# A second order list for attention and feed-forward products: 384 and 512 tokens instead of 448 and 448

## The chip, the cores and the metric

The kernel runs on one core of a Trainium2 chip. The time is device time in microseconds (us) of one execution, from the start of the program to its end; of several executions the median is given. TensorE is called PE here, VectorE DVE, ScalarE ACT, GpSimd POOL and SyncE SP, as the profile calls them.

## The reference

Three layers follow one another, all in float32, for 2 batches of 448 tokens.

```python
# causal attention: 12 heads, 448 tokens, 64 dims
scores = matmul(q, k.T) / sqrt(64);  scores[upper triangle] = -1e9
attn = exp(scores - max);  attn = attn / (sum(attn) + 1e-9);  a = attn @ v
x = a.transpose(0, 2, 1, 3).reshape(2, 448, 768)
# feed-forward with token mixing
xk = mu_k * x + (1 - mu_k) * x_prev        # x_prev: x one token earlier
xr = mu_r * x + (1 - mu_r) * x_prev
x = sigmoid(xr @ w_r) * (maximum(xk @ w_k, 0) ** 2 @ w_v)   # 768 -> 1024 -> 768
# convolution feed-forward
h = maximum(x @ w_in, 0)                   # 768 -> 1024
out = (h * sigmoid(conv3(h, conv_w))) @ w_out               # 1024 -> 768
```

## The kernel before

The attention is cut into 12 jobs of two heads each (a head pair): jobs 0 to 5 are batch 0, jobs 6 to 11 batch 1. For a job, q and k are loaded (`Lk`, lines 281 to 286), transposed on PE (`kqT`, L300) and copied out of PSUM (`kC`, L307). The scores come in two parts (`sc`, L321), over row tiles of 64 queries, tile i against (i + 1) * 64 keys. For each of the 7 row tiles, DVE adds the mask and takes the maximum in one custom instruction (`red`, L334), ACT takes the exponential and sums it (`exp`, L343), and after the reciprocal (`rec`, L350 and L351) each tile is scaled (`norm`, on POOL, DVE or ACT). PE transposes p back in two groups a and b (`T`, L363), four copies of 512 columns bring that into SBUF (`C`, L372, on ACT or DVE), and PE multiplies with v (`V`, L391) into a bank called `po`. From `po` the token mixing follows: `mP` scales it by one factor (kind 0 into `mixed`, kind 1 into `m`), `mD` adds the shifted part (DVE), and `mH` and `mL` split the mixed tokens into a high and a low part, `xr`.

Every feed-forward product is three matmuls in a split float32 format, high by high, high by low, low by high (`mm3`, L64). A slice of 128 columns of a weight is loaded as 64-bit numbers (`w1:L`, L159), narrowed to float32 in steps a to e (a on ACT, b on POOL or DVE, the others on DVE), and split into high (`h`, ACT) and low (`l`). `w0` to `w5` are the six slices of w_r and `w6` to `w8` the first three of w_k. `pr e.b.c` is the product of w_r's slice e with the b-th part of the tokens and the c-th 128 rows (L563 to L569); six of them, c = 0 to 5, fill one PSUM bank, which `sr` copies out. `k x:H` and `k x:L` split `mixed` into the parts of `xk`, x = 6 * batch + c. `E0` to `E3` are the products of w_k's first two slices, each with 6 values of c: slice 0 with both parts of the tokens, then slice 1 (L599 to L603).

What sets the order is a list of such tokens, `ORDER` (from L500). It is issued token by token and PE, ACT, DVE and POOL run their instructions in just that order (L625); SP takes its DMAs in it too. A letter behind a slash is the engine: a is ACT, v is DVE, p is POOL. `W0` and `W*n` are matmuls on a constant early on. After the list the rest of the kernel follows (remaining w_k slices, w_v, w_in, convolution, w_out), ordered by the scheduler; its stages already use 512 and 384 columns. Below, the "tail" is the stretch in which only products are left on PE, between the last job's `V` and the end of the list.

Of the kernel before, what the change touches and what calls it, by code (L numbers as in the profile page):

```python
# [19 lines left out]
def kernel(  # L20
# [457 lines left out]
    class Slice:  # L478
# [27 lines left out]
        3:kC.k/a 2:sc.1 0:norm.5/p 0:C.bX/v 0:T.a 1:rec 2:red.6 1:norm.6/p 2:exp.3 3:sc.1 0:C.aX/a 2:exp.2 2:exp.5
        2:red.1 1:norm.0/p 3:sc.2 0:C.aY/v 4:kqT 1:norm.2/p 3:red.6 1:norm.5/p 2:exp.0 2:red.4 1:norm.4/p 2:exp.1
        1:norm.1/p 1:T.a 3:red.5 Wend 4:kC.k/v 3:red.0 w1:L 1:C.aY/v 2:exp.4 1:Lv 2:exp.6 1:norm.3/p 2:rec 3:exp.0
        0:V.b 1:T.b 4:kC.q/a 3:exp.6 2:norm.5/p 2:norm.1/p 4:sc.1 3:red.1 2:norm.3/p 3:exp.5 0:V.a 3:red.3 1:C.bY/v
        2:norm.6/p w1:a 2:norm.0/p 2:norm.2/p w1:b/p 3:red.2 3:red.4 1:C.bX/v 1:C.aX/v 4:red.4 3:exp.3 2:norm.4/p  # L510
        0:mP.1/a 5:Lk 3:exp.4 4:red.1 2:T.a 3:exp.2 4:sc.2 2:T.b 3:exp.1 0:mP.0/v 2:C.aX/a 4:red.6 2:C.aY/a 3:rec
        w1:c 3:norm.3/p 3:norm.0/p 5:kqT 4:exp.1 4:red.3 4:red.0 2:C.bX/v 4:exp.4 5:kC.k/v 0:mD.1 3:norm.5/p
        3:norm.1/p 4:red.2 1:V.a 5:kC.q/a 4:exp.0 1:V.b 5:sc.2 4:exp.3 4:red.5 4:exp.6 3:norm.2/p 3:norm.6/p 6:Lk
        0:mD.0 3:norm.4/p 5:red.0 0:mH/p 2:Lv 0:mL/p 6:kqT 5:red.2 2:C.bY/a 5:red.3 4:exp.5 5:red.5 7:Lk 3:Lv
        6:kC.q/a 3:T.a 4:exp.2 3:T.b 5:sc.1 3:C.aY/v w1:d 4:rec 6:kC.k/a 3:C.aX/a 3:C.bY/a 1:mP.1/a 4:norm.4/p
# [5 lines left out]
        3:mP.0/v w1:l/p 7:sc.2 9:Lk 7:sc.1 5:T.a 7:red.0 5:C.aY/a 6:exp.2 7:red.6 3:mD.1 7:red.5 6:exp.4 4:V.b
        5:norm.1/p 4:V.a 8:kqT 6:exp.0 7:exp.6 7:red.1 pr1.0.0 w2:L 3:mD.0 3:mH/p 6:rec pr1.0.1 7:red.4 2:mH/p
        6:norm.4/p 5:T.b 8:kC.q/a 7:red.2 7:exp.0 6:norm.5/p 5:C.aX/a 8:kC.k/a 7:red.3 4:mP.1/v 6:norm.6/p 9:kqT
        5:C.bY/v 7:exp.1 6:norm.0/p 9:kC.q/a 4:mP.0/a 5:C.bX/v 7:exp.5 7:exp.3 9:kC.k/v 8:sc.1 7:exp.2 8:red.6
        2:mL/p 8:sc.2 6:norm.1/p 6:T.a 8:red.3 5:V.a 8:red.4 3:mL/p 8:red.2 5:V.b w2:a 6:C.aY/v 6:norm.2/p 7:exp.4
        6:C.aX/a 6:norm.3/p 8:exp.6 4:mD.1 6:T.b 8:red.1 10:Lk 8:exp.2 4:mD.0 7:rec 8:exp.1 w2:b/p 7:norm.6/p w2:c
        10:kqT 8:red.5 pr1.0.2 10:kC.q/a 6:C.bX/a 8:red.0 w2:d 8:exp.0 7:norm.0/v pr1.0.3 4:mH/a 6:C.bY/a 7:norm.5/a
        9:sc.1 w2:e 6:Lv w2:h 10:kC.k/v 11:Lk 9:sc.2 9:red.5 9:red.6 5:mP.1/v 4:mL/p w2:l/p w3:L 8:exp.4 6:V.b 6:V.a
        8:exp.5 7:T.a 8:exp.3 9:red.3 9:red.2 9:red.1 7:norm.2/p 7:norm.1/p w0:L 5:mP.0/a 8:rec 7:C.aY/a pr1.0.4
        9:exp.5 9:exp.6 7:norm.4/v 5:mD.1 6:mP.1/a w3:a 5:mH/p pr2.0.0 5:mL/p 7:norm.3/v 8:norm.4/v pr2.0.1 9:red.0  # L530
# [533 lines left out]
```

## Time and profile before

| | us |
|---|---|
| median of three runs (354.3, 354.36, 353.45) | 354.3 |
| the profiled execution, its span | 351.6 |
| PE busy in it | 345.2 |
| DVE busy | 306.9 |
| ACT busy | 235.1 |
| POOL busy | 90.3 |

The profile is of one execution; its span is the time from its first to its last instruction, and all times in the rows are counted from its start. An engine is busy when an instruction of it runs; time in which it waits is idle time. Matmuls overlap in PE's pipeline, so its busy time counts overlapping ones once. Two rows that follow one another on an engine overlap a little too, so the price of an instruction in a full engine is the distance from its start to the next start.

### The profile page before, as it was taken

What the parts mean: (1) busy time and instruction counts of PE and PEld (TensorE: products, weight loads), DVE (VectorE), ACT (ScalarE), POOL (GpSimd) and SP (SyncE); (2) the same over time, 40 slices, a digit from 0 to 9 for tenths busy, and PEclk for the clock granted to TensorE, in tenths of its full rate; (3) what the DMA queues carried; (4) which work ended last, traced back from release to release, by engine and by line L of the source; (5) the groups of instructions that cost most, each with busy time, mean ns of one, the idle gap of its engine ahead of it and who ended that gap; (6) DMA issues with size and microseconds to landing.
All of it is one profiled execution on the core that took longest, in us unless ns stands there. A gap on an engine that the chain in (4) does not pass through costs nothing.

```text
span 351.6 us, 7196 instructions
## 1 busy us (share of the span) xinstructions
PE 345.2 (98%) x2682; PEld 309.2 (88%) x2682; DVE 306.9 (87%) x629; ACT 235.1 (67%) x515; POOL 90.3 (26%) x149
## 2 busy tenths in 40 slices
...
GB/s 132 146 222 144 127 222 213 90 116 93 7 95 106 66 180 181 121 148 240 142 187 171 156 101 173 179 143 128 89 103 79 89 2 0 67 134 202 138 91 135
DMA packets 63228, 45.33 MB, mean 129 GB/s; under 512 B 34752, under 2 KB 62156, under 8 KB 63192
## 3 DMA queue, kind: packets, MB, share of 16 engines
...
q10 hardware_dynamic: 928, 0.23, 0.3%
...
## 4 chain that ended last, share of the span: by engine, by line
PE 95%; DVE 1%; DMA 1%; POOL 1%; SPq 1%; issue 1%; ACT 0%; POOLq 0%
PE pk L66 17%; PE pv L66 17%; PE pr L66 13%; PE A L66 7%; PE po L391 6%; PE s L321 4%; PE B L66 4%; PE c L66 2%; PE Yb L363 2%; PE D L66 2%; PE Xa L363 2%; PE W L561 1%; PE q L300 1%; PE ph5l L66 1%; PE ph6l L66 1%; PE ph4l L66 1%
## 5 line engine op out<-in xcount | busy, mean ns | idle before, releaser
L887 POOL DMA_DIRECT2D s<-g x12 | 12.7, 1177 | 194.9 <-ACT st L87 188.6
L343 ACT ACTIVATE p<-e,st 128x448 f32<-128x448 f32 (+6 forms) x84 | 42.1, 507 | 1.7 <-DVE st L334 1.5
L72 POOL TENSOR_SCALAR p<-p,st 128x64 f32<-128x64 f32 (+6 forms) x70 | 34.6, 512 | 20.7 <-DVE st L334 11.4
L334 DVE CUSTOM_DVE_ANT_0 e<-s,mask 128x192 f32<-128x192 f32 (+6 forms) x84 | 31.6, 415 | 0.4 <-ACT p L343 0.2
L391 PE MATMUL po<-pt,v 128*64 128x128 f32 (+4 forms) x384 | 24.0, 277 | 0.0
L807 DVE SCALAR_TENSOR_TENSOR cv<-hT,cw,cv 128x448 f32<-128x448 f32 x32 | 21.5, 681 | 2.7 <-ACT cv L804 2.6
L391 PEld LDWEIGHTS po<-pt,v 128*64 128x64 f32 x384 | 20.0, 137 | 3.3 <-issue 0.3
L321 PE MATMUL s<-kT,qT 64*64 64x384 f32 (+6 forms) x336 | 22.1, 386 | 0.5 <-DVE kT L79 0.2
L321 PEld LDWEIGHTS s<-kT,qT 64*64 64x64 f32 x336 | 14.9, 132 | 6.6 <-ACT qT L79 0.7
L343 ACT ACTIVATION_READ_ACCUMULATOR p<-e,st 128x1 f32 x84 | 16.3, 194 | 0.0
L91 POOL TENSOR_TENSOR xr<-m,xr 128x448 fp32r<-128x448 f32 x10 | 12.0, 1198 | 2.1 <-ACT xr L87 1.7
L87 ACT ACTIVATE x<-xv 128x512 fp32r<-128x512 f32 (+1 forms) x12 | 6.8, 573 | 8.1 <-DVE xv L706 8.0
L811 ACT ACTIVATE cv<-cv 128x448 f32<-128x448 f32 x16 | 9.1, 571 | 3.2 <-DVE cv L807 3.2
L999 ACT ACTIVATE o<-A 128x384 f32<-128x384 f32 x3 | 1.5, 491 | 14.7 <-PE A L66 14.6
L804 ACT ACTIVATE cv<-hT,cw 128x448 f32<-128x448 f32 x16 | 10.7, 668 | 0.5 <-DVE g L91 0.3
L813 DVE TENSOR_TENSOR cv<-cv,hT 128x448 f32<-128x448 f32 x16 | 9.9, 621 | 1.2 <-ACT cv L811 1.2
L91 DVE TENSOR_TENSOR k<-a,k 128x512 fp32r<-128x512 f32 (+2 forms) x16 | 9.9, 619 | 0.0
L66 PE MATMUL pv<-k,wv0hl 128*128 128x512 f32 (+1 forms) x48 | 9.9, 364 | 0.0
L66 PE MATMUL pv<-k,wv4hl 128*128 128x512 f32 (+1 forms) x48 | 9.8, 363 | 0.0
L66 PE MATMUL pv<-k,wv2hl 128*128 128x512 f32 (+1 forms) x48 | 9.8, 363 | 0.0
L66 PE MATMUL pv<-k,wv3hl 128*128 128x512 f32 (+1 forms) x48 | 9.8, 363 | 0.0
L66 PE MATMUL pv<-k,wv5hl 128*128 128x512 f32 (+1 forms) x48 | 9.8, 363 | 0.0
...
## 6 DMA issues: line engine op xcount, KB each, us to landing
rqk<-in_q_dram SPq DMA_DIRECT2D x24, 112.0 KB, 2.8
rqk<-in_k_dram SPq DMA_DIRECT2D x22, 112.0 KB, 3.0
...
```

The lines of the kernel that those rows point to most:

```text
L66: nc.tensor.matmul(ps_out, x, y, start=first and i == 0, stop=last and i == 2, skip_group_check=more,)
L72: nc.gpsimd.tensor_scalar(out_, in_, s, 1.0, ALU.mult, ALU.mult)
L91: e.tensor_tensor(out_, x, f32(h), ALU.subtract)
L321: nc.tensor.matmul(held[self.name(f"s{f}")][1][h, o:z], qT[r, i * LO:(i + 1) * LO], kT[r, :(i + 1) * LO], start=True, stop=True,)
L334: nc.vector.tensor_tensor_reduce(t[:, :w], used(self.name(f"s{f}"))[:, o:z], mask[:, S - w:], -SCALE, 3e38, ALU.add, ALU.min, self.st[:, 0 ...
L343: nc.scalar.activation(p[:, :w], self.s[i][:, :w], AF.Exp, bias=self.st[:, 0, i:i + 1], scale=-1.0, accum_out=self.st[:, 1, i:i + 1],)
L363: nc.tensor.transpose(o[:, u * LO:(u + 1) * LO], self.p[i][r, k0:k0 + P], ident[r, r])
L391: nc.tensor.matmul(self.T["po"][j * D:(j + 1) * D, 1 + i * LO - z:1 + (i + n) * LO], self.v[:, kc, j], self.T["pt"][:, a - z:a + n * LO], ...
L804: nc.scalar.activation(a, x[:, 0:S], AF.Copy, scale=cw[:, f:f + 1])
L807: nc.vector.scalar_tensor_tensor(a, x[:, j:S + j], cw[:, j * NF + f:j * NF + f + 1], a, ALU.mult, ALU.add)
L813: (nc.gpsimd if eng == "p" else nc.vector).tensor_tensor(a, a, hc, ALU.mult)
L887: nc.gpsimd.dma_start(out=dst, in_=f32(x), accum_op=ALU.add)
```

## The change

The order list is replaced by another of the same 712 pieces of work: the same loads, scores, exponentials, products. What differs is their order and, for copies, scalings, mixing and splitting steps, the engine that does them. Job 9 now comes ahead of jobs 7 and 8. Each product of w_r and the two slices of w_k now takes tokens 0 to 383 (part 0) and 384 to 895 (part 1) instead of 448 and 448, and so do the copies `sr` and the first two w_k slices' squares. The E products run as E2, E0, E3, E1 instead of E0, E1, E2, E3. The first weight load, `w1:L`, stands behind job 5's `Lk` instead of in front of it.

```diff
     TOK = [slice(b * S, (b + 1) * S) for b in range(B)]
+    PART = [slice(0, 3 * P), slice(3 * P, NT)]
+
+    def width(t):
+        return t.stop - t.start
...
     ORDER = """
...
-        11:norm.6/p 11:norm.1/v 11:norm.5/a 10:C.aY/a 9:V.a 9:V.b 11:norm.4/p 11:norm.0/a 7:mH/p 10:C.bX/v 11:T.b
...
+        11:norm.2/p 11:norm.1/p 11:T.b 11:C.bY/a 11:C.bX/a 10:V.a w5:d w5:e w7:L 10:V.b 10:mP.1/a 10:mD.1 11:V.a
...
     def xr_products(e, b, c):
         if c == 0:
             bank(f"pr{e}_{b}", 1)
-        products(held[f"pr{e}_{b}"][1][:, :S], [slices[e].t], xr, TOK[b], NC, c)
+        t = PART[b]
+        products(held[f"pr{e}_{b}"][1][:, :width(t)], [slices[e].t], xr, t, NC, c)
...
-        copy(eng, sr[e][:, TOK[b]], used(f"pr{e}_{b}")[:, :S])
+        t = PART[b]
+        copy(eng, sr[e][:, t], used(f"pr{e}_{b}")[:, :width(t)])
...
             f, b = divmod(int(what[1:]), B)
-            pk_banks[f, b] = bank(f"pk{f}_{b}", 1)[:, :S]
+            t = PART[b]
+            pk_banks[f, b] = bank(f"pk{f}_{b}", 1)[:, :width(t)]
             for c in range(NC):
-                products(pk_banks[f, b], [slices[NE + f].t], [xk[i] for i in range(NC)], TOK[b], NC, c)
+                products(pk_banks[f, b], [slices[NE + f].t], [xk[i] for i in range(NC)], t, NC, c)
...
-        pks = [(TOK[b], pk_banks[f, b]) for b in range(B)] if f < 2 else token_mm(f"pk{f}", w, xk, False)
+        pks = [(PART[b], pk_banks[f, b]) for b in range(B)] if f < 2 else token_mm(f"pk{f}", w, xk, False)
```

Three places show how the instructions stand. The first is ACT at the end of the attention, in the kernel before; `p5_1` is a tile of probabilities that is scaled, `pt` the transposed p, `Xa_11` the PSUM bank of job 11's group a, `wr5c` a weight slice in step a, `m` and `mixed` the mixed tokens, `xr2` a high part.

```order
L76 ACTIVATE p5_1_137<-p5_1_137,st_144 128x384
L79 COPY pt_0_140<-Ya_10_1817 128x512
L76 ACTIVATE p0_1_121<-p0_1_121,st_144 128x64
L137 ACTIVATE wr5c_1900<-wr5raw_1735 128x768
L87 ACTIVATE xr2_108<-m_8_1730 128x448
L76 ACTIVATE m_9_1922<-po_9_1860,mu_98 128x448
L137 ACTIVATE wr4c_1926<-wr4raw_1750 128x768
L76 ACTIVATE mixed3_103<-po_9_1860,mu_98 128x448
L79 COPY pt_1_141<-Xa_11_1904 128x512
L76 ACTIVATE m_11_1976<-po_11_1950,mu_98 128x448
```

The same place on ACT after the change:

```order
L76 ACTIVATE p0_1_121<-p0_1_121,st_144 128x64
L76 ACTIVATE p6_1_139<-p6_1_139,st_144 128x448
L79 COPY pt_1_141<-Ya_10_1837 128x512
L79 COPY pt_1_141<-Xa_10_1836 128x512
L79 COPY pt_1_141<-Xb_10_1858 128x512
L79 COPY pt_1_141<-Yb_10_1859 128x512
L137 ACTIVATE wr5c_1887<-wr5raw_1735 128x768
L79 COPY pt_0_140<-Ya_11_1895 128x512
L79 COPY pt_0_140<-Xa_11_1894 128x512
L79 COPY pt_0_140<-Yb_11_1917 128x512
L79 COPY pt_0_140<-Xb_11_1916 128x512
L76 ACTIVATE m_10_1957<-po_10_1936,mu_98 128x448
```

All eight copies of the last two jobs are ACT's now, where five of them were DVE's, and the mixing steps and a weight step stand elsewhere.

The second place is SP's queue in the kernel before, around the first weight load; `rqk_4` are job 4's q and k, `v_1` is one of the buffers of v.

```order
L286 DMA rqk_4_393<-in_q_dram 64x7x64 x2
L286 DMA rqk_4_393<-in_k_dram 64x7x64 x2
L159 DMA wr1raw_517<-in_moe_w_r_dram 128x6x128
L292 DMA v_1_113<-in_v_dram 128x3x64 x2
L293 DMA v_1_113<-in_v_dram 64x2x64
L286 DMA rqk_5_602<-in_q_dram 64x7x64 x2
L286 DMA rqk_5_602<-in_k_dram 64x7x64 x2
```

The same place on SP after the change:

```order
L290 DMA rqk_4_450<-in_q_dram 64x7x64 x2
L290 DMA rqk_4_450<-in_k_dram 64x7x64 x2
L290 DMA rqk_5_461<-in_q_dram 64x7x64 x2
L290 DMA rqk_5_461<-in_k_dram 64x7x64 x2
L159 DMA wr1raw_639<-in_moe_w_r_dram 128x6x128
L296 DMA v_1_113<-in_v_dram 128x3x64 x2
L297 DMA v_1_113<-in_v_dram 64x2x64
```

Job 5's four issues for q and k went ahead of the weight load and of v's three.

The third place is PE at the first products, in the kernel before; `q_8` and `k_8` are job 8's transposes, `Yb_5` and `Xb_5` job 5's of p, `pr1_0` the bank of w_r's slice 1 and the first part of the tokens.

```order
L300 MATMUL q_8_1093<-ident_85,rqk_8_945 128x64
L300 MATMUL k_8_1094<-ident_85,rqk_8_945 128x64
L66 MATMUL pr1_0_1113<-xr0_106,wr1hl_971 128x448 x3
L66 MATMUL pr1_0_1113<-xr1_107,wr1hl_971 128x448 x3
L363 MATMUL Yb_5_1131<-ident_85,p1_1_125 128x64
L363 MATMUL Xb_5_1130<-ident_85,p1_1_125 128x64
```

The first products on PE after the change:

```order
L367 MATMUL Ya_7_1370<-ident_85,p6_1_139 128x64
L66 MATMUL pr1_0_1390<-xr0_106,wr1hl_1116 128x384 x3
L66 MATMUL pr1_0_1390<-xr1_107,wr1hl_1116 128x384 x3
L66 MATMUL pr1_0_1390<-xr2_108,wr1hl_1116 128x384 x3
L66 MATMUL pr1_0_1390<-xr3_109,wr1hl_1116 128x384 x3
L66 MATMUL pr1_0_1390<-xr4_110,wr1hl_1116 128x384 x3
L66 MATMUL pr1_0_1390<-xr5_111,wr1hl_1116 128x384 x3
L367 MATMUL Yb_7_1427<-ident_85,p1_1_125 128x64
L367 MATMUL Xb_7_1426<-ident_85,p1_1_125 128x64
```

The products of slice 1 with the first part were two tokens here and the other four further on; now all six stand together, later in the list, inside job 7's transposes of p.

## Rows read from the trace of the kernel before

**Rows 1.** The page: busy time of each engine, share of the span, instructions.
```profile
PE 345.2 (98%) x2682; PEld 309.2 (88%) x2682; DVE 306.9 (87%) x629; ACT 235.1 (67%) x515; POOL 90.3 (26%) x149
```

**Rows 2.** Windows: busy time per engine, granted clock, DMA share; from:to and length first.
```profile
core 0: us, PE busy (x) PEld busy (x) DVE busy (x) ACT busy (x) POOL busy (x), PEclk, DMA share, GB/s
8.23:82.30 74.07, 72.95 (x1158) 59.44 (x1160) 73.12 (x260) 73.13 (x229) 52.80 (x86) 1.00 0.66 164
...
60.41:63.01 2.60, 2.60 (x15) 2.14 (x15) 2.60 (x10) 2.60 (x7) 2.07 (x4) 1.00 1.16 292
...
82.30:88.88 6.58, 6.58 (x136) 5.85 (x138) 5.37 (x12) 6.58 (x13) 5.41 (x10) 1.00 0.01 2
88.88:90.10 1.22, 1.22 (x29) 1.13 (x25) 1.22 (x3) 0.00 (x1) 0.02 (x1) 1.00 0.00 0
90.10:136.20 46.10, 46.10 (x223) 41.90 (x224) 41.07 (x57) 21.88 (x36) 11.27 (x11) 1.00 0.32 103
```

**Rows 3.** PE's longest wait: total us, times, longest.
```profile
PE W L561 <- POOL ident masks.py:199: 1.7, 1, 1.7
```

**Rows 4.** Chain that ended last: start, us, engine, what, matmuls (x).
```profile
90.10 30.57 PE pr L66 x147
120.66 3.72 PE pk L66 x18
...
179.77 58.03 PE pv L66 x288
237.79 4.12 PE ph0l L66 x18
...
318.61 4.16 PE D L66 x24
```

**Rows 5.** Timeline of ACT, end of the attention: start, us, line, operation, tiles.
```profile
83.89 0.62 ACT L76 ACTIVATE p<-p,st 128x384 f32<-128x384 f32 x1
84.42 0.57 ACT L79 COPY pt<-Ya 128x512 f32<-128x512 f32 x1
84.88 0.35 ACT L76 ACTIVATE p<-p,st 128x64 f32<-128x64 f32 x1
85.13 0.93 ACT L137 ACTIVATE wr5c<-wr5raw 128x768 f32<-128x768 f32 x1
85.97 0.56 ACT L87 ACTIVATE xr<-m 128x448 fp32r<-128x448 f32 x1
86.43 0.62 ACT L76 ACTIVATE m<-po,mu 128x448 f32<-128x448 f32 x1
86.95 0.94 ACT L137 ACTIVATE wr4c<-wr4raw 128x768 f32<-128x768 f32 x1
```

**Rows 6.** Timeline of DVE in the tail.
```profile
96.40 0.67 DVE L416 SCALAR_TENSOR_TENSOR mixed<-po,mu,mixed 128x448 f32<-128x448 f32 x1
97.00 0.61 DVE L91 TENSOR_TENSOR xr<-m,xr 128x448 fp32r<-128x448 f32 x1
97.53 0.92 DVE L142 TENSOR_SCALAR wr5c<-wr5c 128x768 int32<-128x768 int32 x1
98.37 0.61 DVE L91 TENSOR_TENSOR xk<-mixed,xk 128x448 fp32r<-128x448 f32 x1
```

**Rows 7.** Groups of POOL's instructions, low parts: busy us, mean ns, idle before.
```profile
L91 POOL TENSOR_TENSOR xk<-mixed,xk 128x448 fp32r<-128x448 f32 x3 | 4.8, 1608 | 2.8 <-ACT xk L87 2.8
```

**Rows 8.** Timeline of SP's queue: issues of the first weight load and job 5's k.
```profile
16.82 0.62 SPq L159 DMA_DIRECT2D wr1raw<-in_moe_w_r_dram  x1
...
21.10 1.85 SPq L286 DMA_DIRECT2D rqk<-in_k_dram  x2
```

**Rows 9.** The page: issues of k, KB each, median us from issue to landing.
```profile
rqk<-in_k_dram SPq DMA_DIRECT2D x22, 112.0 KB, 3.0
```

**Rows 10.** Timeline of PE: the first transpose of job 5.
```profile
27.20 0.27 PE L300 MATMUL q<-ident,rqk 64*128 64x64 f32 x1
```

**Rows 11.** Timeline of ACT: the last exponential of job 3.
```profile
26.21 0.39 ACT L343 ACTIVATE p<-e,st 128x128 f32<-128x128 f32 x1
```

More of the change, by code (lines that the diff above doesn't have):

```diff
@@ L506 @@
[L506 to L515, printed above, removed]
@@ L521 @@
[L521 to L530, printed above, removed]
@@ L546 @@
-        9:mL/p pr3.1.0 11:mH/a w5:b/v w4:e 10:mL/v pr1.1.3 k4:H/a 11:mD.0 10:mD.0 11:mL/v w5:c pr2.1.2 k0:H/p
-        pr3.0.4 pr1.1.4 k2:H/a pr1.1.5 k6:H/p w4:h k1:L/v w5:d pr2.1.3 k11:H/p k8:H/a pr2.1.4 w4:l/v k6:L/v w6:L
-        pr0.1.3 pr0.1.4 k7:H/a pr3.1.1 k0:L/v pr2.1.5 pr4.1.0 pr4.0.0 w5:e w5:h pr3.1.2 w5:l/v 9:mD.0 pr3.1.3
-        pr4.0.1 pr4.1.1 w6:a k3:H/p k5:H/a pr3.1.4 pr4.1.2 pr4.1.3 k5:L/v w7:L pr5.1.0 k7:L/p pr0.1.5 w6:b/p pr5.1.1
-        sr1.1/a pr4.0.2 w6:c w6:d k9:H/p pr5.0.0 pr5.1.2 k10:H/a k4:L/v w7:a w6:e w7:b/v k2:L/v pr3.0.5 w7:c pr5.0.1
@@ new lines @@
+        6:C.bX/a 5:V.b 7:norm.1/p 7:norm.2/p 6:C.bY/a 8:red.2 8:exp.3 5:mP.1/a 7:norm.5/a 4:mP.0/v 8:red.4
+        8:exp.4 8:red.0 7:norm.3/p 4:mD.0 8:red.5 6:V.a 8:exp.0 w2:a 5:mD.1 8:exp.2 8:red.1 5:mP.0/v 9:red.4
+        6:V.b 6:mP.1/a 11:Lk 10:kqT 10:kC.k/v 7:T.a 10:kC.q/a 5:mD.0 pr1.0.0 pr1.0.1 pr1.0.2 5:mH/p 5:mL/v
+        8:exp.5 pr1.0.3 pr1.0.4 pr1.0.5 w2:b/p w2:c 9:red.1 7:C.aX/a 7:C.aY/a 8:exp.1 w2:d 9:exp.6 7:norm.4/p
+        w2:e 8:rec 8:norm.5/p 7:T.b 7:C.bY/a 7:C.bX/a 6:mP.0/a 9:exp.4 11:kqT 9:sc.2 9:red.5 9:exp.5 11:kC.q/v
@@ new lines @@
+        7:V.a 7:V.b 10:sc.1 w2:h sr1.0/v 9:red.2 9:red.0 9:exp.0 11:kC.k/a 9:red.3 8:norm.0/p 6:mD.1 8:norm.2/p
+        6:mD.0 10:red.4 8:norm.6/p 10:red.1 9:exp.3 10:sc.2 10:red.6 8:norm.3/a 9:Lv 9:exp.2 8:T.a 8:norm.1/p
+        8:Lv w3:L 10:red.3 9:exp.1 10:Lv 9:rec 10:red.0 w3:a 8:norm.4/p 8:T.b 8:C.bX/v 10:exp.6 8:C.aX/v
+        10:exp.3 w2:l/p pr2.0.0 7:mP.1/v 9:norm.5/a 10:exp.4 6:mH/p pr2.0.1 pr2.0.2 pr2.0.3 pr2.0.4 9:norm.0/p
+        10:exp.1 8:C.bY/v 9:norm.2/p pr2.0.5 w0:L 9:norm.1/p 10:red.5 10:red.2 9:norm.4/p 9:norm.6/p 7:mP.0/v
@@ new lines @@
+        pr3.1.0 11:rec 10:norm.1/a 11:norm.5/a 11:norm.3/a pr3.0.4 11:norm.0/a 7:mL/p pr1.1.1 11:norm.6/a 8:mD.0
+        9:mP.0/v 10:norm.6/p pr3.1.1 9:mD.0 10:T.a 10:C.aY/a 10:C.aX/a w0:d w0:e 10:T.b 10:C.bX/a 9:mL/v 8:mH/p
+        8:mL/p pr3.0.5 11:norm.4/p w4:L 10:C.bY/a w5:a w5:b/v pr3.1.2 w5:c 11:T.a 11:C.aY/a 11:C.aX/a
+        11:norm.2/p 11:norm.1/p 11:T.b 11:C.bY/a 11:C.bX/a 10:V.a w5:d w5:e w7:L 10:V.b 10:mP.1/a 10:mD.1 11:V.a
+        w0:h 11:V.b 11:mP.1/a 10:mH/a w0:l/v act2 k1:H/a 11:mD.1 11:mH/a pr2.1.0 pr2.1.1 pr2.1.2 10:mL/v pr2.1.3
```

68 lines of the change are left out of this document (41 added, 27 removed).

## The prediction

> **What bounds the kernel now.** I read the view by stages first, then what TensorE (PE) waits for, the chain of waits, and the timelines of the engines around the end of the attention. All durations are of the one profiled execution, 351.6 us [rows 1]; the median of the three timed runs is 354.3 us, 2.7 above it, and I carry a difference found in the profile to that median unchanged. About 0.3%, 1.06 us, is what a measurement of this kernel can tell from no change.
>
> The page gives PE 98% [rows 1], which by itself would say that PE sets everything. The stages say more [rows 2]. From the first exponential (8.23 us) to the end of the last one (82.30), a stretch of 74.07 us, PE, VectorE (DVE) and ScalarE (ACT) are busy 72.95, 73.12 and 73.13 us: three engines take turns with under 1.2 us of idle time each, so none of them alone is the limit. From 82.30 to 88.88 ACT is busy 6.58 of 6.58 us and DVE 5.37: there ACT's list is what ends last. From 88.88 to 90.10 ACT does nothing; PE runs the last pair's products with v. From 90.10 to 136.20 PE is busy 46.10 of 46.10 us and ACT 21.88: the tail is pure PE. PE's waits are almost nothing, the only one over 0.3 us is 1.7 us at the very start [rows 3]. In the attention its matmuls overlap and their ends are modelled, so a busy PE may hide waiting. [...]
>
> [...]
>
> **Widths.** In the chain a matmul 448 columns wide takes 3.72/18 = 206.7 ns (w_r's in the tail 30.57/147 = 208), one of 512 4.12/18 = 229 ns, one of 384 4.16/24 = 173 ns [rows 4]. The w_v stage, which alternates 384 and 512, gives 58.03/288 = 201.5 ns. So a pair 384+512 costs 402 to 403 ns, a pair 448+448 413.4. The change turns 144 pairs (36 of w_r's products, 12 of the two w_k tiles, three matmuls each) from the one into the other: 144 x 11.4 = 1.6 us of PE less.
>
> Where it falls: before, 22 product tokens stand ahead of the last pair's products with v: 66 x 206.7 = 13.6 us. After, 23 do, 18 of 384 and 5 of 512: 54 x 173 + 15 x 229 = 12.8 us. Behind it before 222 x 206.7 = 45.9 us, after 18 tokens of 384 (9.3), 31 of 512 (21.3) and the four E (14.5) = 45.1. So 0.8 us goes out of the PE-bound tail and counts in full; 0.8 us goes out of the attention, where it counts only if PE sets the pace.
>
> [...]
>
> **The list on ACT.** I counted what ACT does up to its last copy of a transposed p. More after the change: copies of 512 columns 29 to 34, at 0.46 each (start to start, 84.42 to 84.88 [rows 5]) +2.3; scalings of p 4 to 9, namely three more of 256 columns (estimate 0.43, between 0.25 for 64 and 0.53 for 384 [rows 5]), two of 384, one of 64, one of 192 less (0.37, the same estimate): +2.2. Less: one scaling of the mixed tokens (0.52) -0.5; two steps 768 wide (0.84 each) -1.7; two high parts of xr (0.46) -0.9; two sr copies of 448 against one of 384 -0.5. Sum +0.9 us of ACT ahead of the last pair's products with v. Copies of q and k change places with DVE, four for four, at nothing.
>
> **The list on DVE and POOL.** Up to the last reciprocal DVE loses six scalings of p (0.25 to 0.5 by ACT's prices, -2.4), two conversion steps and a low part of a weight, each 768 wide (0.84 each, 97.53 to 98.37 [rows 6], -2.5), and gains two mixes and two scalings of the mixed tokens (0.60 each, 96.40 to 97.00, +2.4) and two low parts of xr (0.53, +1.1): about -1.4 us. It also loses five of its 19 copies of p. POOL takes on eight more low parts of xk in the tail, 1.6 us each while DVE works beside it [rows 7], +13 us: POOL has 11.27 us of work in the 46.10 of the tail [rows 2], so there is room, and I cost it at nothing. If that cover failed, the last low part, k11, would be late for the last block of E3, which starts 21 x 229 ns = 4.8 us ahead of the end of E1: nothing to 2 us.
>
> **First weight load.** w1's load was issued at 16.82 us ahead of pair 5's q and k, whose last issue begins at 21.10 and lasts 1.85 [rows 8], to 22.95; with the median 3.0 us from issue to landing [rows 9] they were there at about 25.9. PE's transposes of pair 5 start at 27.20 [rows 10], 1.3 us later. Taking the load's 0.62 us of issue from in front of them gains nothing, since nothing waited for them. The load itself comes some 3.6 us later, about 20.4, and by the same 0.62 and 3.0 lands at about 24. Its first conversion, on ACT, stands behind the last exponential of pair 3 now; in before that pair's last one begins at 26.21 and lasts 0.39 [rows 11], so at that pace the data is 2.6 us early. I take 0; the ends are -0.6 (the issue time in full) and, if pair 3 is done 3 us sooner after the change, +0.4.
>
> **Sum.** The last pair's products with v end at 90.10 in before; ACT's list sets that, from 8.23 to 88.88. ACT's idle in the first stretch is 0.94 us [rows 2]. If the new list leaves the same idle time, those 80.65 us become 81.6, the tail begins 0.9 us later and is 0.8 us shorter: +0.1. If it leaves none: -0.8. If DVE is what paces and not ACT, its 1.4 us less let the first stretch end earlier, but ACT's own work allows no more than that -0.8. If the new list idles 1 us longer: +1.1. The early part (what the exponentials of the first two pairs find ready) I could only bound, -0.4 to +0.4. I take the nearest row, the same idle time: +0.1, so 351.7 in the profile and 354.4 on the median; with half of the idle time gone, 353.9. The forecast is 354.2.
>
> **Rivals.**
> (A) *Forecast: the same, ACT and DVE pace the attention, the tail gives its 0.8 back.* For it: the stretch 82.30 to 88.88 [rows 2]. Own range 353.2 to 355.2. Chance 0.46.
>
> (B) *PE paces the whole kernel and its saving comes out in full.* For it: PE's 72.95 of 74.07 and no waits. Price: -0.8 ahead, -0.8 in the tail, and product runs between narrow attention matmuls fall from six to four, at most 0.1 each: -1.6 to -2.0, so 352.5. Against: ACT's full 6.58 us before the tail. Chance 0.25.
>
> (C) *Slower: the products now come in blocks.* Before, the first products on PE are two tokens in a row, 6 x 206.7 ns = 1.2 us; after, pr1.0.0 to pr1.0.5 and pr2.0.0 to pr2.0.5 go as 18 matmuls in a row, 18 x 173 = 3.1 us, ahead of pair 7's transposes and pair 9's scores. If DVE and ACT drain what is ready within the block, each block leaves both idle for up to 1 us. Two such blocks and ACT's added 0.9: +0.9 + 2 - 0.8 = +2.1, so 356.4. It decides when ACT's idle time from its first exponential to its last copy of p is over 1.9 us. Against: a run of 12 matmuls, 60.41 to 63.01, already stands in before and leaves ACT and DVE busy 2.60 of 2.60 [rows 2]. Chance 0.23.
>
> (D) *Widths save nothing* (the tail's 448 wide matmuls are no slower per column than the others): the terms of 0.8 vanish, +0.9 with the same idle time, so 355.2, at the edge of slower. Against: the three durations of rows 4. Chance 0.06.
>
> **How the numbers follow.** Faster by over 0.3%: B and 0.05 of A, its best end: 0.30. Slower: C and half of D: 0.26. Within 0.3%: the rest of A and of D, 0.44. The range goes from B's 352.5 to C's 356.4; what lies outside is a B that also shortens the start (0.1) and a C with more than two blocks (0.1); by these ends it is 352.4 to 356.4.
>
> **What would show it.** The profile after: widths right if 384 and 512 alternate at 173 and 229 ns from the last pair's products to the end of E1 and that stretch takes about 45.1 us without a wait; ACT's term right if its busy time from first exponential to last copy of p is 0.9 us up; the move of w1 right if nothing on ACT or PE waits for pair 5's q, k or for w1. The forecast is wrong if PE has gaps behind the last products with v (the last pair's low part of xr is needed five tokens of 512, 3.4 us, after them; its scaling, mix, high and low part take 0.52 + 0.60 + 0.46 + 0.53, with one weight step of 0.84 between them on DVE, 2.95 together), or if ACT stands idle during the blocks (rival C), or if the last products with v end before 89 us (rival B).

## The result: 0.6% slower

The changed kernel takes 356.41 us (median of four runs, 355.69 to 357.14), the kernel before 354.33 (353.45 to 354.75): ratio 1.006, 95% interval 1.004 to 1.008. The forecast was no change, 354.2 us. In a second series the ratio was 1.0082 (1.0058 to 1.0106).

One thing about the two profiles first. In the profiles taken since, an execution's time is its span plus 1.7 to 2.1 us (356.65 against 354.8 for the changed kernel). The span of 351.6 us that the prediction starts from therefore belongs to an execution of about 353.45 us, the fastest of the three shown, and of the 2.7 us from it to the median some 0.8 are only that. I use a second profile of the same kernel below, "before again", 354.31 us with a span of 352.5.

The page of the changed kernel, busy time of each engine, answers to [rows 1]:

```profile
PE 344.9 (97%) x2682; PEld 307.7 (87%) x2682; DVE 297.6 (84%) x607; ACT 243.0 (69%) x530; POOL 99.5 (28%) x156
```

The windows of the changed kernel answer to [rows 2]. They are cut at the first exponential, the end of the last one, the end of the last product with v, the end of the E products, and the end:

```profile
9.45:83.84 74.39, 70.65 (x1175) 58.82 (x1170) 72.62 (x256) 73.16 (x231) 53.28 (x92) 1.00 0.59 149
83.84:92.84 9.00, 8.54 (x139) 6.94 (x137) 8.32 (x12) 8.52 (x18) 3.20 (x8) 1.00 0.28 89
92.84:138.27 45.43, 45.43 (x221) 40.09 (x221) 32.36 (x43) 26.62 (x45) 22.28 (x15) 1.00 0.32 105
138.27:354.78 216.51, 212.61 (x1092) 195.12 (x1091) 182.35 (x291) 132.60 (x235) 17.36 (x20) 1.00 0.43 126
```

The same cuts in before again:

```profile
9.13:83.18 74.05, 72.78 (x1156) 59.29 (x1158) 73.08 (x259) 73.11 (x229) 52.87 (x86) 1.00 0.64 162
83.18:91.01 7.83, 7.83 (x161) 7.01 (x161) 6.64 (x14) 6.61 (x13) 5.43 (x11) 1.00 0.01 2
91.01:137.07 46.06, 46.06 (x223) 41.86 (x224) 40.91 (x57) 21.89 (x36) 11.28 (x11) 1.00 0.32 104
137.07:352.53 215.46, 212.09 (x1093) 195.20 (x1091) 184.39 (x294) 131.47 (x235) 17.35 (x20) 1.00 0.44 127
```

Read the lengths first: from the first exponential to the last product with v 83.39 us instead of 81.88 (+1.51), the tail 45.43 instead of 46.06 (-0.63), the part behind the list 216.51 instead of 215.46 (+1.05). With the first exponential 0.32 us later, 9.45 against 9.13, this makes the 2.25 us between the two spans; that start differs from one execution to the next, from 8.2 to 9.8 us in the profiles of this case. Then read PE's busy time, the first number behind the length, in the first two rows: PE is idle 74.39 - 70.65 + 9.00 - 8.54 = 4.20 us in the attention, where it was 1.27. Its work there is 1.42 us less; its waits are 2.93 us more.

PE's longest waits, answering to [rows 3] (total us, times, longest), are new small ones ahead of the scores and the transposes ("pair" is a job, as in the prediction); the first is ahead of pair 1's scores, 1.16 us up to 11.54, for DVE's copy of q. Not all of it is loss: these scores start 2.09 us behind the first exponential here and 1.75 in before again.

```profile
PE s L325 <- DVE qT L79: 1.5, 2, 1.2
PE Yb L367 <- DVE mixed L420: 0.4, 1, 0.4
```

The widths cost what [rows 4] said: 18 matmuls of 384 columns take 3.12 us (126.79 to 129.91), 173 ns each, 18 of 512 take 4.12 (129.91 to 134.03), 229 ns each:

```profile
126.79 3.28 PE L66 MATMUL pk<-xk,wk0hl 128*128 128x384 f32 x18
129.91 4.28 PE L66 MATMUL pk<-xk,wk1hl 128*128 128x512 f32 x18
134.03 4.24 PE L66 MATMUL pk<-xk,wk0hl 128*128 128x512 f32 x18
```

And the first block of 18 products, rival C's place, leaves nobody idle; window of the changed kernel, DVE and ACT busy 3.11 of 3.11 us (in the second block, 69.11 to 72.34, 3.20 and 3.23 of 3.23):

```profile
58.71:61.82 3.11, 3.11 (x18) 3.08 (x18) 3.11 (x8) 3.11 (x9) 1.75 (x3) 1.00 0.50 106
```

The prediction's own mark was ACT from its first exponential to its last copy of p, which ends at 91.55:

```profile
83.84:91.55 7.71, 7.25 (x120) 5.90 (x120) 7.07 (x11) 7.25 (x17) 3.20 (x8) 1.00 0.21 64
```

With the first row above ACT is busy 80.41 of 82.10 us, where [rows 2] give 79.71 of 80.65. Its work is 0.70 us more (forecast 0.9), its idle time 1.69 instead of 0.94 (forecast the same, and over 1.9 for rival C).

### The profile page after: what moved, and what is told of

The parts are those of the page before. It is cut to its first block, busy times and chain, and to the rows that moved or that the text cites. A ratio compares the mean times of both kernels' runs of the same rounds, so it can differ in the third digit from the quotient of the medians.

```text
span 354.8 us, 7202 instructions
## 1 busy us (share of the span) xinstructions
PE 344.9 (97%) x2682; PEld 307.7 (87%) x2682; DVE 297.6 (84%) x607; ACT 243.0 (69%) x530; POOL 99.5 (28%) x156
## 4 chain that ended last, share of the span: by engine, by line
PE 41%; DVE 23%; DMA 17%; ACT 12%; issue 4%; POOL 2%; SPq 0%; ACTq 0%; POOLq 0%; DVEq 0%
PE A L66 7%; DVE e L338 4%; PE B L66 4%; PE pr L66 3%; ACT p L347 3%; PE po L395 2%; PE c L66 2%; PE s L325 2%; PE D L66 2%; PE W L568 1%; DMA wk5raw<-in_moe_w_k_dram 1%; DMA wv3raw<-in_moe_w_v_dram 1%; DMA wv2raw<-in_moe_w_v_dram 1%; DMA wv1raw<-in_moe_w_v_dram 1%; DMA wv5raw<-in_moe_w_v_dram 1%
## 5 line engine op out<-in xcount | busy, mean ns | idle before, releaser
L347 ACT ACTIVATE p<-e,st 128x320 f32<-128x320 f32 (+6 forms) x84 | 42.7, 522 | 2.4 <-DVE st L338 2.4
L72 POOL TENSOR_SCALAR p<-p,st 128x320 f32<-128x320 f32 (+6 forms) x72 | 33.6, 486 | 25.7 <-DVE st L355 18.4
L338 DVE CUSTOM_DVE_ANT_0 e<-s,mask 128x320 f32<-128x320 f32 (+6 forms) x84 | 31.7, 414 | 1.5 <-PE s L325 0.7
L325 PE MATMUL s<-kT,qT 64*64 64x448 f32 (+6 forms) x336 | 22.3, 386 | 1.5 <-DVE qT L79 1.5
L91 POOL TENSOR_TENSOR xk<-mixed,xk 128x448 fp32r<-128x448 f32 x11 | 16.2, 1497 | 6.2 <-ACT xk L87 6.2
L347 ACT ACTIVATION_READ_ACCUMULATOR p<-e,st 128x1 f32 x84 | 17.7, 211 | 0.0
L91 DVE TENSOR_TENSOR k<-a,k 128x384 fp32r<-128x384 f32 (+1 forms) x16 | 9.8, 619 | 0.7 <-ACT k L87 0.7
L367 PE MATMUL Yb<-ident,p 64*128 64x64 f32 x96 | 8.2, 226 | 1.9 <-DVE mixed L420 0.4
L79 DVE COPY qT<-q 128x448 f32<-128x448 f32 x7 | 4.2, 606 | 6.9 <-PE k L304 6.9
L367 PEld LDWEIGHTS Yb<-ident,p 64*128 64x128 f32 x96 | 6.8, 138 | 3.6 <-issue 2.3
```

The source lines that it names most:

```text
L72: nc.gpsimd.tensor_scalar(out_, in_, s, 1.0, ALU.mult, ALU.mult)
L91: e.tensor_tensor(out_, x, f32(h), ALU.subtract)
L325: nc.tensor.matmul(held[self.name(f"s{f}")][1][h, o:z], qT[r, i * LO:(i + 1) * LO], kT[r, :(i + 1) * LO], start=True, stop=True,)
L338: nc.vector.tensor_tensor_reduce(t[:, :w], used(self.name(f"s{f}"))[:, o:z], mask[:, S - w:], -SCALE, 3e38, ALU.add, ALU.min, self.st[:, 0 ...
L347: nc.scalar.activation(p[:, :w], self.s[i][:, :w], AF.Exp, bias=self.st[:, 0, i:i + 1], scale=-1.0, accum_out=self.st[:, 1, i:i + 1],)
L367: nc.tensor.transpose(o[:, u * LO:(u + 1) * LO], self.p[i][r, k0:k0 + P], ident[r, r])
```

## The experiments

Ratios are against runs of the kernel before on the same chip, with 95% intervals. The attention's length is from the first exponential to the last product with v, in the one profiled execution of each kernel. "Behind the list" is the stretch from the end of the E products to the end of the program.

**Both kernels again.** No edit.

> The kernel before, unchanged, for a second profile. Theory (the profile of before caught one of its fastest starts): first exponential at about 9.1 us instead of 8.23, last product with v at about 91.0 instead of 90.10, and the stretch from the end of the E products to the end of the program again 215.4 us. Rival (the new list is late at the start by itself): first exponential again at 8.2 us.

> The changed kernel, unchanged, with more rounds. Theory: ratio 1.006; in a second profile the stretch from the first exponential to the last copy of transposed p is again about 82.1 us (before 80.65), products behind the last v 45.4 (before 46.1), and the stretch from the end of the E products to the end 216.5 us (before 215.4), because these come from the order of instructions. Rival (one of these is chance of the run): that stretch falls back to the number of before.

Before again: ratio 1.0 (0.9984 to 1.0016), first exponential at 9.13, attention 81.88 us (81.87 in the first profile), behind the list 215.46 (215.44). So the early start of the first profile was chance, and the rest repeats within 0.02 us. Changed kernel again: tail 45.43 and behind the list 216.50 repeat too; the attention does not, 84.89 against 83.39. That difference comes from loads. The first exponential is 0.60 us earlier, a wait of 0.54 us for pair 4's k takes most of that back, and 1.32 us sit at 24 us. PE's transposes of pair 5 started at 23.22 in the first profile, and the k they need was issued from 17.42 to 18.72, before the weight load (SP's queue, answering to [rows 8]):

```profile
17.42 1.30 SPq L290 DMA_DIRECT2D rqk<-in_k_dram  x2
18.76 0.62 SPq L159 DMA_DIRECT2D wr1raw<-in_moe_w_r_dram  x1
```

PE's timeline, answering to [rows 10]; nothing waits:

```profile
23.22 0.23 PE L304 MATMUL q<-ident,rqk 64*128 64x64 f32 x1
```

In the second execution an issue of v took 3.12 us instead of 1.15, and all behind it came 1.7 us later (SP's queue):

```profile
11.19 3.12 SPq L296 DMA_DIRECT2D v<-in_v_dram  x2
...
19.08 1.30 SPq L290 DMA_DIRECT2D rqk<-in_k_dram  x2
```

PE then stood, mid-pair, until the last k came:

```profile
23.02 0.24 PE L304 MATMUL q<-ident,rqk 64*128 64x64 f32 x1
...
24.58 0.24 PE L304 MATMUL k<-ident,rqk 64*128 64x64 f32 x1 [1.32 <-ACT p L347]
```

The bracket names ACT, but ACT had long been done. The second of the two issues of that k began at about 19.7, 4.9 us before PE went on. In the first profile transfers of q and k issued from 16 to 26 us took 2.5 to 4.0 us to land, in that of before, over the whole kernel, up to 5.5; so I put the wait down to the DMA. The new list leaves this k no less time than the old one: 4.5 us from the end of its issue to its need in the first profile (18.72 to 23.22), 4.25 in before (22.95 to 27.20 [rows 8, 10]). What was late is that one issue of v. Waits of about 1 us for a k stand in single executions of both lists: 1.08 us in before_more_act, 1.24 in list_only.

**The widths and the list apart.** widths_only runs the old list with the new widths (E products in its order); list_only runs the new list with 448 and 448.

```
widths_only:  ORDER = """ <list of before> """   # code of the changed kernel
list_only:    ORDER = """ <new list> """         # code of the kernel before
```

> The old list with 384 and 512 tokens in the products of w_r and the first two w_k tiles. Theory (ACT and DVE pace the attention, the tail is PE): the stretch behind the last product with v 0.7 us shorter, the attention unchanged, so ratio 0.998, about 353.6 us. Rival 1 (the widths bring the loss behind the list, through the order of what follows): that stretch 1.1 us longer, ratio 1.001. Rival 2 (PE paces the attention too): 1.6 us less, ratio 0.9955.

> The new list, with 448 and 448 tokens as before. Theory (the list costs some 1.5 us on ACT in the attention and 1.1 us behind the list, and the widths give 0.7 back): ratio 1.0077, about 357.0 us, with the last product with v where the changed kernel has it, and a tail of 46.1 us. Rival (the widths bring the loss behind the list): ratio 1.004.

widths_only: ratio 1.0008 (0.9993 to 1.0024), so neither the gain of the theory nor PE's full gain. list_only: 1.01 (1.0068 to 1.0131), above its theory, but its profiled execution has that wait of 1.24 us in its attention of 85.62. The windows of widths_only, attention and tail, show where the gain stayed:

```profile
8.86:90.58 81.72, 79.48 (x1315) 65.78 (x1315) 79.44 (x273) 79.67 (x241) 58.55 (x96) 1.00 0.58 148
90.58:137.42 46.84, 46.84 (x223) 40.86 (x224) 40.26 (x56) 21.60 (x36) 11.32 (x11) 1.00 0.31 99
```

PE has 1.13 us less work in the attention (79.48 against 80.61), but the attention is only 0.16 shorter: the time turns into waiting. And the tail is 0.78 us longer, since the old list puts the first, now narrow, halves of w_r's products ahead of it and leaves the wide halves in it. The loss behind the list does not come with the widths either: that stretch is 215.41 us in widths_only and 217.02 in list_only. The slower part of the change is the list.

**The order behind the list.** Behind the list a scheduler orders the work. PE loses the time at one place there: from its first w_in product to the second tile's first it takes 5.23 us (239.69 to 244.92) instead of 4.13 (237.63 to 241.76 in before). On DVE the step b of w_in's fifth tile (`wi4c`) stands ahead of the last w_v tile's product with its sigmoid (`xv`). DVE in the changed kernel:

```profile
238.63 0.95 DVE L146 SCALAR_TENSOR_TENSOR wi3c<-wi3raw,wi3c 128x768 int32<-128x768 int32 x1
240.60 0.56 DVE L140 TENSOR_SCALAR wi4c<-wi4c 128x768 f32<-128x768 f32 x1 [1.02 <-ACT wi4c L137]
...
242.14 0.68 DVE L716 TENSOR_TENSOR xv<-pv,sr 128x512 f32<-128x512 f32 x1
...
243.60 0.68 DVE L91 TENSOR_TENSOR x<-xv,x 128x512 fp32r<-128x512 f32 x1
```

DVE waits 1.02 us for that step's data while xv could run (the edit below shows it), and PE's first w_in products wait for what follows from xv:

```profile
243.54 0.50 PE L66 MATMUL ph0l<-x,wi0hl 128*128 128x512 f32 x1 [0.24 <-ACT x L87]
244.34 0.74 PE L66 MATMUL ph0l<-x,wi0hl 128*128 128x512 f32 x2 [0.30 <-DVE x L91]
```

In before the step stands ahead of xv too, but it waits 0.32 us, and xv follows at once (DVE):

```profile
234.78 0.56 DVE L140 TENSOR_SCALAR wi4c<-wi4c 128x768 f32<-128x768 f32 x1 [0.32 <-ACT wi4c L137]
235.26 0.68 DVE L706 TENSOR_TENSOR xv<-pv,sr 128x512 f32<-128x512 f32 x1
```

What differs more is the load of that tile, `wi4raw`. Its issue stands 8.3 us ahead of PE's first w_in product in before (229.33 to 237.63), 7.0 in before again, 4.6 in the changed kernel (235.12 to 239.69). Why the loads come later there was not traced.

The edit ties that step behind xv on DVE and nothing else:

```diff
+            xv_ = nc.vector.tensor_tensor(a, pv, sr[e][:, t], ALU.mult)
...
+            tc.add_manual_dep(x.ins, xv_.ins.name, <order only>)   # x: i4:b
```

> The changed kernel; on DVE the first product of the last w_v tile with its sigmoid (xv5) goes ahead of the step b of w_in's fifth tile, where the kernel before has it. Theory (this order, which the scheduler chose behind the list, costs 1.04 to 1.07 us): the stretch from the end of the E products to the end of the program falls from 216.5 to 215.4 us, the rest is unchanged, time 1.0 us below the changed kernel's. Rival (the weight conversions are late there whatever the order): less than 0.3 us.

355.64 us, ratio 1.0041 (1.0028 to 1.0055), against 1.006 and 1.0082 for the changed kernel. Behind the list it is 215.35 us, as in before, though before has no such order; DVE:

```profile
237.35 0.95 DVE L152 SCALAR_TENSOR_TENSOR wi3c<-wi3raw,wi3c 128x768 int32<-128x768 int32 x1
238.22 0.68 DVE L722 TENSOR_TENSOR xv<-pv,sr 128x512 f32<-128x512 f32 x1
239.25 0.56 DVE L141 TENSOR_SCALAR wi4c<-wi4c 128x768 f32<-128x768 f32 x1 [0.35 <-ACT wi4c L138]
```

So 1.1 us of the profile's loss came from a stage that the change does not touch, and this order takes it away. It does not follow that the order alone costs 1.1 us; see the next experiment.

**The first weight load and pair 5.** after_w1_first puts the load back in front; after_v_later instead gives pair 5 more room; after_xv5_v joins that with the edit on xv.

```diff
after_w1_first
-1:norm.6/p 5:Lk 4:kqT        ... 3:norm.1/p w1:L 2:T.b
+1:norm.6/p w1:L 5:Lk 4:kqT   ... 3:norm.1/p 2:T.b
after_v_later
-2:sc.2 1:exp.2 1:Lv 3:kqT    ... 1:norm.6/p 5:Lk 4:kqT
+2:sc.2 1:exp.2 3:kqT         ... 1:norm.6/p 5:Lk 1:Lv 4:kqT
```

> The changed kernel with the first weight load back in front of pair 5's q and k. Theory (the new list needs these q and k at about 23.1 us instead of 27.2, and they land between 20.5 and 24.0): they come 0.6 to 0.7 us later and PE waits for them in more of the runs; 0.3 to 0.7 us above the changed kernel. Rival (the step of the prediction: nothing waits there): no difference.

> The changed kernel with pair 1's v loaded behind pair 5's q and k instead of ahead of pair 3's and 4's work. Theory (in part of the runs PE waits for pair 5's q and k): they land some 1.8 us earlier, PE's wait there is gone, 0.5 to 1.3 us below the changed kernel. Rival (v is late in their place, PE waits for it in pair 1's products with v, about 24.7 us): no gain or a loss.

> Both edits in the changed kernel. Theory: the gains add, 1.5 to 2.3 us below the changed kernel, so within 0.3% of the kernel before (354.4 to 355.5 us). Rival: only one of them shows.

after_w1_first: 359.43 us, 1.0151 (1.0135 to 1.0167), 1.9 to 3.0 us above the changed kernel, more than either theory had. PE's timeline in it has two waits, 1.37 us together:

```profile
24.60 0.24 PE L304 MATMUL q<-ident,rqk 64*128 64x64 f32 x1 [0.80 <-DVE st L338]
25.41 0.34 PE L304 MATMUL k<-ident,rqk 64*128 64x64 f32 x1 [0.57 <-DMA rqk<-in_k_dram]
```

The larger part is the clock. Behind these waits the granted clock is 0.50, up to about 31.6 us:

```profile
25.20:31.60 6.40, 6.19 (x57) 4.54 (x57) 2.63 (x10) 3.60 (x10) 2.60 (x6) 0.50 0.64 145
```

Pair 4's scores and pair 1's products with v fall into it. Here, and then in the changed kernel, where the granted clock is 1.00 from 23.83 to 26.65:

```profile
26.31 1.77 PE L325 MATMUL s<-kT,qT 64*64 64x448 f32 x12
28.01 3.69 PE L395 MATMUL po<-pt,v 128*64 128x256 f32 x32
...
23.83 0.99 PE L325 MATMUL s<-kT,qT 64*64 64x448 f32 x12
24.74 1.98 PE L395 MATMUL po<-pt,v 128*64 128x256 f32 x32
```

From start to start they take 1.70 and 3.62 us (the next scores start at 31.63) instead of 0.91 and 1.91 (26.65): 2.5 us. PE had stood idle 0.80 and 0.57 us with one transpose between before the clock fell, and had run without a wait since 25.41 when it rose. All four executions of this kernel have a mean granted clock of 0.990 to 0.995; of the changed kernel's eight, seven have 0.999 or 1.000, and one, the slowest of its series with 357.14 us, has 0.995. The wait of 1.32 us in the second profile of the changed kernel left the clock at 1.00. What makes it fall was not tried.

after_v_later: 355.86, 1.0049 (1.0035 to 1.0062), without a wait for pair 5's q and k. But its attention, 83.46 us, is that of the changed kernel's first profile (83.39), which did not wait there either; what its profile gains is behind the list, 215.56 us. So the theory's gain is not shown. after_xv5_v: 355.64, 1.0040 (1.0027 to 1.0052): the two do not add.

Behind the list after_v_later loses only 0.1 us and after_w1_first nothing (215.48), though both have the changed kernel's order there. DVE in after_v_later:

```profile
238.95 0.56 DVE L140 TENSOR_SCALAR wi4c<-wi4c 128x768 f32<-128x768 f32 x1 [0.84 <-ACT wi4c L137]
```

Their load of that tile is issued 5.4 and 5.5 us ahead of PE's first w_in product, not 4.6 (4.5 in the changed kernel's second profile, which loses 1.04). The loss is made by the order and a load as late as that together. What is left of after_xv5_v against before, 1.4 us by the ratio, is the attention: 83.48 us against 81.88, with the tail 0.6 shorter.

**Single waits and moved work, on after_xv5_v as the base.** fix_rec also moves pair 8's high part (`8:mH`, on POOL) forward, since the low part needs it.

```diff
fix_mix
-1:mP.0/v 3:exp.5 3:exp.3 3:rec 1:mD.0 ... 3:norm.3/p 1:mP.1/a
+3:exp.5 3:exp.3 1:mP.1/a 1:mP.0/v 3:rec 1:mD.0 ... 3:norm.3/p
fix_rec
-9:mD.0 10:T.a ... 8:mH/p 8:mL/p pr3.0.5
+9:mD.0 8:mH/p 8:mL/v 10:T.a ... pr3.0.5
fix_act
-7:norm.5/a ... 8:norm.3/a ... 9:norm.5/a
+7:norm.5/p ... 8:norm.3/p ... 9:norm.5/p
```

> The changed kernel with both earlier edits (xv5 first on DVE, pair 1's v behind pair 5's q and k), and pair 1's scaling of po on ACT ahead of DVE's scaling and mixing of the same po. Theory (ACT stands idle 0.6 us at 28 us because it reads po only when DVE is done with it): that idle time goes, 0.6 us off, about 355.0. Rival (the wait only moves to DVE): no change, 355.6.

> The same base; pair 8's low part of xr on DVE behind pair 9's mixing instead of on POOL. Theory (the last pair's sum step on DVE, 0.87 us instead of 0.17, cannot run while POOL subtracts, and ACT and PE wait 0.45 us for it): the step takes 0.2 us, the two waits go, 0.4 us off. Rival (DVE is as full as POOL there): no change or 0.3 more.

> The same base; three of ACT's scalings of p (two of 384, one of 256, together 1.4 us) on POOL. Theory (ACT paces the attention, so its added work is paid in full): the last exponential 1.0 to 1.4 us earlier, time 1.0 to 1.4 us off, as good as the kernel before. Rival (PE or DVE paces it): under 0.4 us.

> All five edits together. Theory: 2.0 to 2.4 us below the base's 355.64, so 353.2 to 353.7, faster than the kernel before by 0.7 us or more. Rival (they share one cover): no better than the best of the three alone.

fix_mix: 1.0029 (1.0018 to 1.004), perhaps 0.4 us better than the base, but the intervals overlap, and its attention is 83.52 us, as on the base. ACT's 0.61 us of idle time became 0.25 and 0.19, and DVE got a wait of 0.69: the wait moved, as the rival had it. fix_rec: 1.0018 (1.0007 to 1.0028), 0.8 us better by the ratios (the intervals just touch), and its attention is 82.91 us, 0.57 shorter. On the base, DVE's sum step of the last pair ended as POOL's subtraction did:

```profile
83.93 0.86 DVE L360 TENSOR_SCALAR st<-st 128x7 f32<-128x7 f32 x1 [0.18 <-ACT p L353]
```

POOL on the base, 83.42 to 84.76:

```profile
83.42 1.34 POOL L91 TENSOR_TENSOR xr<-m,xr 128x448 fp32r<-128x448 f32 x1
```

With the subtraction elsewhere the step takes 0.17 us (DVE in fix_rec):

```profile
83.38 0.17 DVE L360 TENSOR_SCALAR st<-st 128x7 f32<-128x7 f32 x1 [0.19 <-ACT p L353]
```

fix_act: 1.0074 (1.0058 to 1.0091), 1.2 us slower than the base: ACT's idle time grew from 1.74 to 4.10 us, in waits for PE and DVE, and PE itself waited 0.47 and 0.28 us for p, which now came late from POOL. fix_all: 1.0067 (1.0053 to 1.008), with the same waits of PE. Moving the work says nothing on whether ACT paces, since it brings new waits.

**What paces the attention.** Two kernels do more work than before, two leave work out of the base.

```diff
before_more_act
+            for _ in range(2 if (self.i, w) in ((6, "aX"), (7, "aX"), (8, "aX")) else 1):
                 copy(eng, self.T["pt"][:, o:o + 512], x)
before_more_pe
+            for u, (i, kc) in list(enumerate(UNITS[g])) * (2 if self.i == 8 else 1):
drop_act
-7:norm.5/a ... 8:norm.3/a ... 9:norm.5/a
drop_act_early
+            if (self.i, w) not in ((3, "bX"), (3, "aX"), (4, "aX")):
                 copy(eng, self.T["pt"][:, o:o + 512], x)
```

> The kernel before with three of ACT's copies of transposed p (pairs 6, 7 and 8) made twice, 3 x 0.47 = 1.4 us more on ACT, in the attention's second half. Theory (ACT paces the attention): the last exponential and the last product with v 1.2 to 1.4 us later. Rival (PE or DVE paces it and ACT has room): under 0.5 us later.

> The kernel before with the transposes of pair 8's p made twice, 32 small matmuls, 2 x 0.55 = 1.1 us more on PE at about 65 to 68 us. Theory (from the first products on, some 47 to 58 us, PE paces: it has no idle time there): the last product with v 1.0 to 1.1 us later, ratio 1.003. Rival (ACT and DVE pace the attention to its end and PE has slack): under 0.3 us.

> The changed kernel with xv5 first and pair 1's v later; three of ACT's scalings of p (pair 7's and 9's tile 5, pair 8's tile 3) are left out, 1.4 us less on ACT and no other engine gets them. Theory (ACT paces the attention, and the 1.3 us that the same scalings cost on POOL came from POOL being late): last product with v 1.0 to 1.4 us earlier, 354.3 to 354.7. Rival (ACT's work is not what paces it): under 0.4 us.

> The changed kernel with xv5 first and pair 1's v later; three of ACT's copies of transposed p (two of pair 3, one of pair 4, 1.4 us of ACT between 36 and 46 us) are left out, so these pairs' products with v use old data. Theory (before the first products ACT and DVE pace, and PE waits for them, 3.3 us in all): the last product with v 0.7 to 1.4 us earlier, PE's idle time as much less. Rival (DVE paces there, or the loads): under 0.4 us.

before_more_act: 1.0017 (0.9996 to 1.0038), unclear; in its profile the attention is 84.22 us, 2.3 longer, but PE's wait of 1.08 us for pair 8's k is part of that. What ACT's work is worth in the kernel before stays open. before_more_pe: 1.0027 (1.0013 to 1.0042), 1.0 us, and the attention is 1.02 us longer. The two were not measured as one sum: the profiled execution is one of the faster ones (354.44 us, median 355.18), and its tail is 0.87 us shorter than in before, for which see the last section. Its window:

```profile
9.14:92.04 82.90, 81.88 (x1347) 67.39 (x1347) 80.25 (x273) 79.85 (x241) 58.20 (x97) 1.00 0.56 144
```

The base, after_xv5_v:

```profile
9.41:92.89 83.48, 79.25 (x1312) 65.81 (x1306) 81.03 (x268) 81.74 (x247) 56.68 (x99) 1.00 0.56 143
```

drop_act, 1.0041 (1.0026 to 1.0056):

```profile
9.79:93.28 83.49, 79.22 (x1312) 65.77 (x1306) 81.04 (x268) 80.67 (x244) 56.71 (x99) 1.00 0.56 143
```

drop_act_early, 1.0047 (1.0035 to 1.0059):

```profile
8.94:92.29 83.35, 79.23 (x1312) 65.78 (x1306) 80.91 (x268) 80.59 (x244) 56.45 (x99) 1.00 0.56 144
```

ACT's busy time falls by 1.1 us and the attention stays as long, 83.49 and 83.35 against 83.48. The work that is left out turns into idle time. So ACT alone does not pace it under the new list, early or late.

**Versions.** fix_two is the base with fix_mix and fix_rec. tail_widths is the old list with 384 and 512 only where both halves stand in the tail; against the code of the changed kernel:

```diff
-        t = PART[b]
+        t = (PART if e > 3 else TOK)[b]
...
```

> The changed kernel with xv5 first, pair 1's v later, pair 1's scaling of po on ACT first, and pair 8's low part off POOL. Theory (the gains of the single edits, 0.3 and 0.6 us against 1.0040, add): ratio 1.001 to 1.002, so nearly level with the kernel before and still not faster.

> The old list; 384 and 512 tokens only where both halves stand behind the last product with v (w_r's slices 4 and 5 and the two w_k slices), 448 and 448 in slices 0 to 3. Theory (widths pay only in the stretch that PE alone fills, and there only for whole pairs: 72 pairs of 11.4 ns): that stretch 0.8 us shorter than before, 45.2 us, nothing lost in the attention or behind the list; ratio 0.9977. Rival (the 0.6 us that the widths cost in the old list came from waits in the tail, not from the wide halves being left there): no gain.

fix_two: 1.0025 (1.0012 to 1.0038), not better than fix_rec alone; its profile has two waits for loads, 0.83 us on PE and 0.97 on ACT. tail_widths: 353.88 us, 0.9986 (0.9975 to 0.9997): faster than both kernels, than before by 0.5 us, 0.1 to 0.9. Its tail is 0.70 us shorter than before and its attention is not longer:

```profile
8.79:90.77 81.98, 80.58 (x1315) 66.26 (x1315) 79.78 (x273) 79.81 (x241) 58.47 (x97) 1.00 0.58 147
90.77:136.13 45.36, 45.36 (x223) 40.90 (x224) 40.26 (x56) 21.46 (x36) 11.30 (x11) 1.00 0.32 102
```

## Why the prediction was wrong

The forecast was the same time, and it came out 2.1 us slower. In the profiles the forecast's +0.1 became +2.25: the attention +1.51 instead of +0.9, the tail -0.63 instead of -0.8, behind the list +1.05 instead of nothing, the start +0.32, which is chance. By its steps:

- **Widths, 1.6 us of PE.** The durations held (173 and 229 ns). The place did not: "so 0.8 us goes out of the PE-bound tail and counts in full". The tail is 0.63 us shorter, but how much of that the widths give is not settled: list_only, with 448, has a tail of 44.98, shorter still, yet its 448 columns take 202.6 ns and not 206.7; at 206.7 its 222 matmuls would take 45.9. That 448 columns could be that fast, and the widths then save next to nothing, is what rival D said. In the old list the widths put the narrow halves ahead of the tail and lengthen it (widths_only); whole pairs inside the tail paid (tail_widths).
- **"ACT's list sets that."** This is the step that failed. ACT's added work was sized well (+0.70 us up to its last copy, forecast +0.9), but "the same idle time" was not left (1.69 us instead of 0.94), and it is not ACT's work that sets the length: leaving 1.4 us of it out gains nothing (drop_act, drop_act_early), and adding 1.1 us to PE in before costs about 1.0 (before_more_pe), so PE had next to no room there either. With PE, DVE and ACT busy 97 to 98% of before's attention, a saving on one was worth next to nothing (widths_only: 1.13 us off PE, 0.16 off the attention), while work or a wait added to one can cost in full. I priced the list as a sum of work, and what it changed was who waits for whom: PE's idle time in the attention rose by 2.9 us against 1.4 us less work, +1.5.
- **"It gains nothing, since nothing waited for them"** (the first weight load). I took the time at which PE needs pair 5 from the old list, 27.20; the new one needs it at 23.2, and in one execution it waits 1.3 us there even so. With the load back in front, PE waits 1.37 us and behind that its granted clock is 0.50 for 6.4 us, which costs 2.5 more; the time is 1.9 to 3.0 us longer. So within the new list the move is worth more than its 0.62 us of issue, and most of its worth is the clock, for which the prediction's sum has no term.
- **A term that was not in the sum.** I had treated all behind the E products as fixed. The order and the times of the loads there follow from a scheduler and from what the list leaves: +1.05 us, a late load that meets one step on DVE. after_xv5 takes the whole of it away by moving that step. What I wrote ahead of that run, that the kernel before has the two the other way round, is wrong (234.78, then 235.26).
- **The rival that got the number.** C's 356.4 us is the measured time by accident: its blocks leave ACT and DVE busy throughout, and by its own mark it needed 1.9 us of idle time on ACT, where there are 1.69.
- **Rival B's 0.1 us.** No run shows the "at most 0.1 each" for a run of products between narrow matmuls. From the first start of a run to the next start behind it, the six runs of before take 0.13 to 0.19 us more than their number times 206.7 ns (46.27 to 47.68, 1.41 us for six matmuls), the two blocks of the changed kernel 0.21 more than 18 times 173 (58.71 to 62.04, 3.33 us).
- DVE's load was sized wrong as well: -1.4 us forecast up to the last reciprocal, but it is busy 73.48 us instead of 73.24. Part of this are steps that wait for POOL: the twelve sum steps take 3.8 us instead of 2.0.

In the changed kernel five of these twelve steps begin while a splitting step runs on POOL; they take 0.35 to 0.86 us and end 0.02 or 0.03 us behind it. The other seven have no POOL step beside them and take 0.16 to 0.17 us, as the last one does in fix_rec (0.17) without the subtraction. Why DVE's step lasts until POOL's end was not shown.

Not settled: which of the small new waits make the remaining 1.6 us of the attention; 0.57 went with fix_rec. The one at 10.4 us (1.16 us, pair 1's copy of q behind five row maxima) was not taken away, and work was not left out on DVE, whose idle time up to the last product with v (2.4 us on the base) is hardly more than in before (2.2); that DVE paces there is a guess.
